# A parametric activation kept in its PSUM bank, and softmax maxima and sums that pass through PSUM columns

## Chip, cores and metric

One core of a Trainium2 chip runs the kernel. The metric is the device time of one execution in microseconds; 0.2% of it, some 1.7 us, is about what a measurement of this kernel can tell from no change.

The engines are named as the profile names them: PE is TensorE's matmuls, PEld its weight loads, DVE is VectorE, ACT is ScalarE, POOL is GpSimd, SP is SyncE, which here only issues DMAs.

## What is computed

Three stages follow each other on 2304 tokens (4 batches of 576) of 512 values, cut here to what matters:

```python
# 1. attention, 8 heads of 64; heads 0-3 see the last 32 keys, heads 4-7 every 32nd key
scores = scale * q @ k.T ; scores = where(mask, scores, -1e9)
attn = exp(scores - max(scores)) ; attn = attn / (sum(attn) + 1e-9) ; x = attn @ v
# 2. MLP, 512 -> 2048 -> 512, a slope alpha per hidden unit for negative values
h = x @ w_in ; g = maximum(h, 0) + alpha * minimum(h, 0) ; x = g @ w_out
# 3. eight routed experts, 512 -> 1024 -> 512, one expert per token by argmax of the gate
y = relu(x @ w1[e]) @ w2[e] ; out = gate * eom * y
```

## The kernel before

All products are made from fp32 values that are split into two float32r parts, high and low, so that each product is three matmuls (high x high, low x high, high x low).

**Attention.** 48 groups, 12 per batch, each of up to four score tiles ("units") of at most 128 by 128: two pairs of a row tile and a head for groups with 96 or 126 rows, two units for groups with 72 rows. `att_scores` (L218) writes the scores of one head of the pair to the half "S" of a bank and those of the other to another bank; S is columns 0 to 255 of the tile `sl_bank`, which is one PSUM bank of 512 columns. Its other half, "L", is used by the router (`rank`, L618). In the first two batches (`b < PE_MASK`, groups 0 to 23) the mask is added by a matmul and `att_max` (L252) reduces the scores in PSUM to negated maxima `nm`, four numbers a row in SBUF, which L255 multiplies in place by 0.125. In the last two batches (groups 24 to 47) the mask is added on DVE (L258) and the maxima come out of L266 ready. `att_exp` (L280) makes one exponential per unit on ACT, and its accumulator writes the row sums `sm` to SBUF. `att_norm` adds 1e-9 to them (L294), takes the reciprocal (L295), and GpSimd multiplies the tile by it (L296; for group 9 DVE does). Then come transposes (L312), their copy (L314), the product with v (L327) and the split of its result into the MLP's input (L366 on ACT, L371 on DVE).

**MLP.** Six blocks of 384 tokens, 16 pieces of 128 hidden units in each: 96 iterations n of a loop. Iteration n makes the first product of piece n+2 (`mlp_in`, 12 matmuls, L438 to L440, into one of two banks with the tag "h"), its activation (`mlp_act`) and, at its end, its split (`mlp_split`), and the second product of piece n (`mlp_out`, L473 to L475). The activation is two Relu on ACT out of PSUM, of h into `a` and of -h into `bn` (L447, L448, both SBUF), and one DVE instruction a = bn * (-alpha) + a (L449). The split is a copy to float32r on ACT (`gh`, L458) and the difference `gl` = a - gh (L460), on GpSimd in the first block (n < 16) and on DVE afterwards.

**Weights.** They come as float64 and are decoded by integer steps: a scaled copy on ACT (L401), a shift (L405), two shift-and-combine steps on DVE (L406, L412), a float32r copy on ACT (L420) and the difference on GpSimd (L421). 16 weights, five of them decoded beside the first ten attention groups, the rest one per iteration of the first block, for n up to 10.

**Order.** It is written by hand: each engine works through its own queue in program order. First comes a prologue, steps s = 0 to 12 of `att_step` (L1099): exponentials of group s-1, scores of group s (in S for even s, in the "h" banks for odd s), values of s-3, transposes of s-2, maxima of s, normalization of s-1, rest of s-3, then the decoding steps. Then the MLP loop; while it is in block 0 each iteration also holds one attention step (groups 10 to 22), in blocks 1 to 3 about one in two iterations does. Within an iteration the order is: exponentials and normalization of s-1, `mlp_in(n+2)`, values of s-3 and their store, rest, `mlp_act(n+2)`, the end of a decoding (L420, L421), scores and maxima of s, the middle of the next decoding (L405, L406, L412), `mlp_out(n)` with the transposes of s-2 in between, `mlp_split(n+2)`. Semaphores are placed by a framework from the tiles that instructions share. It keeps instructions of different engines on one tile of one PSUM bank in program order, whatever columns they touch: the router's product into columns 256 to 279 of `sl_bank` is given a wait for DVE's read of columns 0 to 255.

After the MLP the experts run (from about 560 us); the change does not touch them.

Of the kernel before, what the change touches and what calls it, by code (L numbers as in the profile page):

```python
# [7 lines left out]
F32 = mybir.dt.float32  # L8
# [4 lines left out]
ALU = mybir.AluOpType  # L13
# [35 lines left out]
SCALE = 0.125  # L49
# Splits ahead of the turn of the tokens of the place after next, by the kinds of three places in a row.  # L50
NB = {"SSP": 0}
XG = 4
XA = 3
# When the parts of the second plan, its lists and its indices come: (place, position).
WHEN = ((0, 7), (1, 1), (1, 1), (1, 4), (1, 6))
OHP = 12
# Groups that VectorE normalizes, and groups whose scores come after matmuls that keep TensorE awake.
NRV = (9,)
FS = {2: 2}
# Parts of the first two products of the MLP that run between the last steps of the first attention.  # L60
PRE = {10: ((0, range(2)),), 11: ((0, range(2, 3)), (1, range(2))), 12: ((1, range(2, 3)),)}
# [22 lines left out]
def attention_prelu_mlp_routed_experts_kernel(  # L84
# [40 lines left out]
    with tc.manual_schedule():  # L125
# [18 lines left out]

# [1 line left out]
        # A visit is a pair of heads of a batch and the groups of its rows that are worked on in turn.  # L146
        visits = [(0, pr, (0, 1) if pr < 2 else (0, 1, 2)) for pr in range(4)]
# [70 lines left out]
        def att_scores(gi, tags):  # L218
# [10 lines left out]
            for ii, j in enumerate(js):  # L229
                q0 = QL * j if local else NP * RS * j  # L230
                k0 = max(q0 - STRIDE, 0) if local else q0
                for h2 in range(2):
# [7 lines left out]
                    )  # L240

        def att_max(gi):
            b, pr, g = groups[gi]
            local, js, r, kk = shape_of(gi)
            nj = len(js)
            nu = 2 * nj
            sc = sc_t[gi]
            pt = apool.tile([P, 4, P], F32, tag="p", name="p", bufs=NP_BUFS)
            nm = apool.tile([P, 4], F32, tag="nm", name="nm", bufs=2)
            if b < PE_MASK:  # L250
                for h2 in range(2):
                    nc.vector.tensor_reduce(  # L252
                        out=nm[:r, h2 * nj : (h2 + 1) * nj], in_=sc[h2][:r, 0:nj, :kk], axis=X, op=ALU.max, negate=True
                    )
                nc.vector.tensor_scalar_mul(nm[:r, :nu], nm[:r, :nu], SCALE)  # L255
            else:
                for h2 in range(2):
                    nc.vector.scalar_tensor_tensor(  # L258
                        out=pt[:r, h2 * nj : (h2 + 1) * nj, :kk],
                        in0=sc[h2][:r, 0:nj, :kk],  # L260
                        scalar=SCALE,
                        in1=masks(gi),
                        op0=ALU.mult,
                        op1=ALU.add,
                    )
                nc.vector.tensor_reduce(  # L266
                    out=nm[:r, :nu], in_=pt[:r, :nu, :kk], axis=X, op=ALU.max, negate=True
                )
            p_t[gi] = (pt, nm)

        def att_exp(gi):
            b, pr, g = groups[gi]
            local, js, r, kk = shape_of(gi)
            nj = len(js)
            sc = sc_t.pop(gi)
            pt, nm = p_t[gi]
            sm = apool.tile([P, 4], F32, tag="sm", name="sm", bufs=3)
            for u in range(2 * nj):
                src = sc[u // nj][:r, u % nj, :kk] if b < PE_MASK else pt[:r, u, :kk]
                nc.scalar.activation(  # L280
                    out=pt[:r, u, :kk],
                    in_=src,
                    func=AF.Exp,
                    bias=nm[:r, u : u + 1],
                    scale=SCALE if b < PE_MASK else 1.0,
                    accum_out=sm[:r, u : u + 1],
                )
            p_t[gi] = (pt, sm)

        def att_norm(gi):  # L290
            local, js, r, kk = shape_of(gi)
            nu = 2 * len(js)
            pt, sm = p_t[gi]
            nc.vector.tensor_scalar_add(sm[:r, :nu], sm[:r, :nu], 1e-9)  # L294
            nc.vector.reciprocal(sm[:r, :nu], sm[:r, :nu])  # L295
            (nc.vector if gi in NRV else nc.gpsimd).tensor_tensor(  # L296
                out=pt[:r, :nu, :kk],
                in0=pt[:r, :nu, :kk],
                in1=sm[:r, :nu].unsqueeze(2).to_broadcast([r, nu, kk]),
                op=ALU.mult,  # L300
            )
# [72 lines left out]

# [1 line left out]
        raw_t, w_t = {}, {}  # L376
# [14 lines left out]

        # A weight comes as a float64, two words; it leaves as the sum of two float32r.
        dec_t = {}
# [48 lines left out]
        def mlp_act(n):  # L442
            c = n % NC1
            ph = h_t.pop(n)
            a = xpool.tile([P, BLK], F32, tag="a", name="a", bufs=2)
            bn = xpool.tile([P, BLK], F32, tag="bn", name="bn", bufs=1)
            nc.scalar.activation(out=a, in_=ph[:, :BLK], func=AF.Relu)  # L447
            nc.scalar.activation(out=bn, in_=ph[:, :BLK], func=AF.Relu, scale=-1.0)  # L448
            nc.vector.scalar_tensor_tensor(  # L449
                out=a, in0=bn, scalar=nalpha[:, c : c + 1], in1=a, op0=ALU.mult, op1=ALU.add  # L450
            )
            h_t[n] = a

        def mlp_split(n):
            a = h_t.pop(n)
            gh = xpool.tile([P, BLK], F32R, tag="gh", name="gh", bufs=3)
            gl = xpool.tile([P, BLK], F32R, tag="gl", name="gl", bufs=2)
            nc.scalar.activation(out=gh, in_=a, func=AF.Copy)  # L458
            eng = nc.gpsimd if n < NC1 else nc.vector
            eng.tensor_tensor(out=gl, in0=a, in1=gh.bitcast(F32), op=ALU.subtract)  # L460
            g_t[n] = (gh, gl)
# [16 lines left out]

# [1 line left out]
        x2_t, lg_t = {}, {}  # L480
# [77 lines left out]
        def route_parts(blk):  # L558
            """One-hot choice, weight and place in its expert's list of each token of a block."""
            lg = lg_t.pop(blk)  # L560
# [75 lines left out]
        def plan_parts(early):  # L636
            """A column is a list of up to 128 tokens of one expert, a place's tokens one or two columns. The
            first EARLY columns hold pairs of full lists of the tokens before the last block. The others
            of each expert come in pairs from C_P on, a last odd one from C_S on; but a last one of FEW
            tokens or less has its column from C_Q on."""  # L640
            k0, k1 = (0, EARLY) if early else (EARLY, NSLOT)
# [206 lines left out]

# [1 line left out]
        # A place is work on one expert: "P" on two columns, "S" on one, "Q" on one of few tokens. "P" makes  # L850
        # the hidden values with the tokens in the free dimension. "Q" takes the weights as they are, its
        # tokens stand in each quarter of the partitions, and each quarter makes its part of a row.
        kinds = ["P"] * (EARLY // 2)
# [13 lines left out]
        def load_expert(t, h, always=False):  # L867
            """The first (h = 0) or second weight of place t's expert, unless it is there already."""
            if t not in regs:
# [190 lines left out]

# [1 line left out]
        load_qk(0)  # L1062
# [36 lines left out]
        def att_step(s, tags, ttag, vtag):  # L1099
            """One step of the attention, each engine's part on what the others did a step ago."""  # L1100
            att_front(s)
# [20 lines left out]
        def decode(k, n):  # L1122
            """The first n steps of a weight's decoding, those that are still to be done."""
            steps = [decode_a, decode_b, decode_s, decode_c]
            for f in steps[steps_done.get(k, 0) : n]:
                f(k)
            steps_done[k] = max(steps_done.get(k, 0), min(n, 4))
# [36 lines left out]
        def gathers(ahead, places=NPL):  # L1164
            """The next tokens, as far as there is room for them."""
            ahead = ahead or len(xg_t) + 1
# [89 lines left out]

# [1 line left out]
        x2T = x2T_tile()  # L1258
# [20 lines left out]
        def split(t, h, some=range(4)):  # L1279
            """Splits, and loads what comes next in the place of what was split."""  # L1280
            if len(some) and t < NPL and kinds[t] != "Q":
# [102 lines left out]
        def some(kind, n, end, step):  # L1384
            """The places of a kind from the n-th on, as far as they are used, step by step."""
            if n < end:
# [105 lines left out]
```

## Time and profile before

| | us |
|---|---|
| three timed runs | 832.44, 833.76, 834.35 (median 833.76) |
| span of the profiled execution, first to last instruction | 831.9 |
| PE busy | 784.2 (94% of the span) |
| DVE, ACT, POOL busy | 478.4, 427.3, 244.5 |

The page gives no other time of the profiled execution than its span: the span lies 0.5 us below the fastest timed run and 1.9 us below the median. A busy time is the sum over an engine's instructions; an instruction that has started and waits for something inside the engine counts as busy. The share of 94% is an average: the first 160 us hold almost all of PE's idle time of the first two stages.

### The profile page before, as it was taken

How to read it: one execution, taken by the hardware profiler on the slowest of the kernel's cores; microseconds unless marked ns; L12 is line 12 of the kernel's file. 1: busy time of each engine (PE TensorE's matmuls, PEld its weight loads, DVE VectorE, ACT ScalarE, POOL GpSimd, SP SyncE). 2: the span in 40 equal slices, each digit the busy share in tenths (PEclk: the TensorE clock that was granted, in tenths of full speed). 3: DMA queues.
4: the chain of work that ended last, by engine and by line, in shares of the span. 5: the costliest groups of instructions: out<-in, count | busy, mean ns of one | idle time of the engine just before them, and what ended most of it. 6: DMA issues, size and time to landing. Idle time of an engine off the chain costs nothing. (4 is left out here: it accounts for less than half of the span.)

```text
span 831.9 us, 13663 instructions
## 1 busy us (share of the span) xinstructions
PE 784.2 (94%) x5032; PEld 659.6 (79%) x5035; DVE 478.4 (58%) x988; ACT 427.3 (51%) x1033; POOL 244.5 (29%) x168
## 2 busy tenths in 40 slices
PE   7687878999999999999999999999989998999995
PEld 4475766788888888888799898889878876878884
DVE  5989999345534554556333424757595447854422
ACT  6756665454455444665433333356534656655542
POOL 2756655200000000110000000032483354546422
PEclk9998999999999999999999999999999999999998
DMA  9716511101200121011000100362224577777421
GB/s 342 298 43 244 190 33 45 44 22 56 84 18 1 47 86 64 1 45 39 1 1 1 39 0 1 149 244 103 77 77 147 194 258 255 285 288 267 161 90 38
DMA packets 22621, 91.04 MB, mean 109 GB/s; under 512 B 3082, under 2 KB 7312, under 8 KB 15376
## 3 DMA queue, kind: packets, MB, share of 16 engines
q1 hardware_dynamic: 18816, 78.52, 26.6%
q0 software_dynamic: 3728, 11.55, 3.9%
q8 instruction: 41, 0.67, 0.3%
q14 instruction: 36, 0.29, 0.1%
HBM read 105.78 MB, written 9.97 MB: 139 GB/s over the span
## 5 line engine op out<-in xcount | busy, mean ns | idle before, releaser
L449 DVE SCALAR_TENSOR_TENSOR a<-bn,nalpha,a 128x384 f32<-128x384 f32 x96 | 73.2, 763 | 116.4 <-ACT bn L448 116.0
L438 PE MATMUL h<-xh,w 128*128 128x384 f32 x384 | 130.4, 340 | 0.4 <-ACT bn L448 0.4
L440 PE MATMUL h<-xh,w 128*128 128x384 f32 x384 | 129.9, 338 | 0.0
L439 PE MATMUL h<-xl,w 128*128 128x384 f32 x384 | 129.7, 338 | 0.0
L296 POOL TENSOR_TENSOR p<-p,sm 96x512 f32<-96x512 f32 (+2 forms) x47 | 48.7, 1036 | 267.6 <-DVE sm L295 255.3
L473 PE MATMUL acc<-w,gh 128*128 128x512 f32 x288 | 126.9, 441 | 0.0
L888 DVE TENSOR_TENSOR wx<-raw,wx 128x1024 fp32r<-128x1024 f32 x72 | 97.1, 1392 | 46.6 <-ACT wx L886 46.3
L475 PE MATMUL acc<-w,gl 128*128 128x512 f32 x288 | 115.8, 402 | 0.3 <-POOL gl L460 0.3
L474 PE MATMUL acc<-w,gh 128*128 128x512 f32 x288 | 115.6, 401 | 0.0
L886 ACT ACTIVATE wx<-raw 128x1024 fp32r<-128x1024 f32 x96 | 94.6, 1056 | 7.3 <-DMA raw<-in_wexp_dram 7.3
L447 ACT ACTIVATE a<-h 128x384 f32<-128x384 f32 x96 | 47.1, 491 | 99.7 <-PE h L440 99.6
L1042 PE MATMUL acc<-wx,hh 128*128 128x512 f32 x304 | 96.8, 400 | 0.0
L888 POOL TENSOR_TENSOR wx<-raw,wx 128x1024 fp32r<-128x1024 f32 x24 | 63.1, 2629 | 89.1 <-ACT wx L886 88.9
L438 PEld LDWEIGHTS h<-xh,w 128*128 128x128 f32 x384 | 73.1, 190 | 5.1 <-ACT bn L448 0.8
L439 PEld LDWEIGHTS h<-xl,w 128*128 128x128 f32 x384 | 72.9, 190 | 4.0
L440 PEld LDWEIGHTS h<-xh,w 128*128 128x128 f32 x384 | 72.6, 189 | 0.0
L895 POOL DMA_INDIRECT xg<-rows,idx_in x23 | 29.4, 1278 | 145.7 <-DVE a L449 139.3
L458 ACT ACTIVATE gh<-a 128x384 fp32r<-128x384 f32 x96 | 49.9, 520 | 42.6 <-DVE a L449 42.5
L475 PEld LDWEIGHTS acc<-w,gl 128*128 128x128 f32 x288 | 55.5, 193 | 14.2 <-POOL gl L460 0.8
L1042 PEld LDWEIGHTS acc<-wx,hh 128*128 128x128 f32 x304 | 56.5, 191 | 11.1
L473 PEld LDWEIGHTS acc<-w,gh 128*128 128x128 f32 x288 | 55.2, 192 | 11.1 <-issue 0.8
L460 DVE TENSOR_TENSOR gl<-a,gh 128x384 fp32r<-128x384 f32 x80 | 44.5, 556 | 28.7 <-ACT gh L458 16.6
(260 smaller groups left out, 1573.7 us busy)
## 6 DMA issues: line engine op xcount, KB each, us to landing
raw<-in_wexp_dram SPq DMA_DIRECT2D x64, 1024.0 KB
raw<-in_wp_dram SPq DMA_DIRECT2D x16, 1024.0 KB
qk<-in_qkv_dram SPq DMA_DIRECT2D x10, 576.0 KB
rows<-stage SPq DMA_DIRECT2D x15, 256.5 KB
v<-in_qkv_dram SPq DMA_DIRECT2D x8, 320.0 KB
qk<-in_qkv_dram SPq DMA_DIRECT2D x4, 384.0 KB
v<-in_qkv_dram SPq DMA_DIRECT2D x6, 256.0 KB
qk<-in_qkv_dram SPq DMA_DIRECT2D x4, 224.0 KB
```

Of the source, the lines that this page charges most:

```text
L296: (nc.vector if gi in NRV else nc.gpsimd).tensor_tensor(out=pt[:r, :nu, :kk], in0=pt[:r, :nu, :kk], in1=sm[:r, :nu].unsqueeze(2).to_broadc ...
L438: mm(ph[:, :BLK], w_in(c, 0, k), xh[:, k, :], start=(k == 0), stop=False)
L439: mm(ph[:, :BLK], w_in(c, 0, k), xl[:, k, :], start=False, stop=False)
L440: mm(ph[:, :BLK], w_in(c, 1, k), xh[:, k, :], start=False, stop=(k == KD - 1))
L449: nc.vector.scalar_tensor_tensor(out=a, in0=bn, scalar=nalpha[:, c : c + 1], in1=a, op0=ALU.mult, op1=ALU.add)
L458: nc.scalar.activation(out=gh, in_=a, func=AF.Copy)
L473: mm(o, gh[:, t], w_out(c, 0), start=(c == 0), stop=False)
L474: mm(o, gh[:, t], w_out(c, 1), start=False, stop=False)
L475: mm(o, gl[:, t], w_out(c, 0), start=False, stop=(c == NC1 - 1))
L886: nc.scalar.activation(out=w[:, :1024], in_=raw, func=AF.Copy)
L888: eng.tensor_tensor(out=w[:, 1024:], in0=raw, in1=w[:, :1024].bitcast(F32), op=ALU.subtract)
L1042: mm(po[i], h[:, h0 : h0 + P], wk[:, w0 : w0 + 512], start=st, stop=sp)
```

## The change

It does two things; beside them it only drops comment lines, so that line numbers stay.

1. In `mlp_act` and `mlp_split`, of -h the Relu writes back into the PSUM bank of h (`v`), the DVE instruction reads v from PSUM and a from SBUF and writes v again, and both steps of the split read v from PSUM. The tile `bn` is gone. The difference `gl` is made on DVE for all pieces. The bank of piece n is so in use until `gl` of piece n is made.
2. A function `few` gives each group four columns for its raw maxima (columns 448 to 479 of `sl_bank`, by group modulo 8) and four for its raw sums (columns 480 to 511). In the first two batches the reductions write there, and the scaling reads there and writes `nm` in SBUF. In all batches the exponentials' accumulators write the sums there, and the addition of 1e-9 reads there and writes `sm` in SBUF.

```diff
+        def few(gi, n):
+
+            c = 448 + 32 * n + 4 * (gi % 8)
+            return sl_bank[:, c : c + 4]
+
         def att_max(gi):
...
             if b < PE_MASK:
+                raw = few(gi, 0)
                 for h2 in range(2):
                     nc.vector.tensor_reduce(
-                        out=nm[:r, h2 * nj : (h2 + 1) * nj], in_=sc[h2][:r, 0:nj, :kk], axis=X, op=ALU.max, negate=True
+                        out=raw[:r, h2 * nj : (h2 + 1) * nj], in_=sc[h2][:r, 0:nj, :kk], axis=X, op=ALU.max, negate=True
                     )
-                nc.vector.tensor_scalar_mul(nm[:r, :nu], nm[:r, :nu], SCALE)
+                nc.vector.tensor_scalar_mul(nm[:r, :nu], raw[:r, :nu], SCALE)
...
-            sm = apool.tile([P, 4], F32, tag="sm", name="sm", bufs=3)
+            sm = few(gi, 1)
             for u in range(2 * nj):
...
-            pt, sm = p_t[gi]
-            nc.vector.tensor_scalar_add(sm[:r, :nu], sm[:r, :nu], 1e-9)
+            pt, raw = p_t[gi]
+            sm = apool.tile([P, 4], F32, tag="sm", name="sm", bufs=3)
+            nc.vector.tensor_scalar_add(sm[:r, :nu], raw[:r, :nu], 1e-9)
             nc.vector.reciprocal(sm[:r, :nu], sm[:r, :nu])
...
             ph = h_t.pop(n)
+            v = ph[:, :BLK]
             a = xpool.tile([P, BLK], F32, tag="a", name="a", bufs=2)
-            bn = xpool.tile([P, BLK], F32, tag="bn", name="bn", bufs=1)
-            nc.scalar.activation(out=a, in_=ph[:, :BLK], func=AF.Relu)
-            nc.scalar.activation(out=bn, in_=ph[:, :BLK], func=AF.Relu, scale=-1.0)
+            nc.scalar.activation(out=a, in_=v, func=AF.Relu)
+            nc.scalar.activation(out=v, in_=v, func=AF.Relu, scale=-1.0)
             nc.vector.scalar_tensor_tensor(
-                out=a, in0=bn, scalar=nalpha[:, c : c + 1], in1=a, op0=ALU.mult, op1=ALU.add
+                out=v, in0=v, scalar=nalpha[:, c : c + 1], in1=a, op0=ALU.mult, op1=ALU.add
             )
-            h_t[n] = a
+            h_t[n] = v
...
-            a = h_t.pop(n)
+            v = h_t.pop(n)
...
-            nc.scalar.activation(out=gh, in_=a, func=AF.Copy)
-            eng = nc.gpsimd if n < NC1 else nc.vector
-            eng.tensor_tensor(out=gl, in0=a, in1=gh.bitcast(F32), op=ALU.subtract)
+            nc.scalar.activation(out=gh, in_=v, func=AF.Copy)
+            nc.vector.tensor_tensor(out=gl, in0=v, in1=gh.bitcast(F32), op=ALU.subtract)
```

## Rows read from the trace of the kernel before

**Rows 1.** Busy time by stretch; per engine us and (instructions), then PEclk, DMA share, GB/s.

```profile
0.00:46.00 46.00, 33.57 (x245) 20.05 (x248) 35.25 (x83) 30.49 (x108) 21.98 (x17) 0.94 0.75 290
...
58.00:142.00 84.00, 68.10 (x389) 53.38 (x388) 82.39 (x107) 52.62 (x144) 49.83 (x31) 0.91 0.38 137
...
160.00:560.00 400.00, 399.37 (x2399) 343.59 (x2398) 190.58 (x536) 184.44 (x539) 31.45 (x31) 1.00 0.13 46
```

**Rows 2.** Groups of DVE instructions by line, 58 to 142 us: busy us, mean ns.

```profile
L406 DVE SCALAR_TENSOR_TENSOR stage<-raw,stage 128x1024 int32<-128x1024 int32 x11 | 21.8, 1982 | 0.4
L449 DVE SCALAR_TENSOR_TENSOR a<-bn,nalpha,a 128x384 f32<-128x384 f32 x11 | 18.3, 1665 | 0.2 <-issue 0.2
L255 DVE TENSOR_SCALAR nm<-nm 96x4 f32<-96x4 f32 (+2 forms) x10 | 16.9, 1692 | 0.3
```

**Rows 3.** Single lines over the whole span: durations in ns, minimum/median/maximum.

```profile
L371 DVE TENSOR_TENSOR xl<-T,xh x56: 168/323/358, 84.1 to 413.7; 128x192 fp32r<-128x192 f32 x20, 128x84 fp32r<-128x84 f32 x12, 128x168 fp32r<-128x168 f32 x12, 128x24 fp32r<-128x24 f32 x6
...
L460 DVE TENSOR_TENSOR gl<-a,gh x80: 546/558/560, 162.3 to 558.9; 128x384 fp32r<-128x384 f32 x80
...
L421 POOL TENSOR_TENSOR w<-stage,w x16: 2342/2582/3347, 23.5 to 142.2; 128x1024 fp32r<-128x1024 f32 x16
```

**Rows 4.** Timeline of one iteration of block 0, DVE and POOL: start, duration.

```profile
107.19 1.23 DVE L412 SCALAR_TENSOR_TENSOR stage<-raw,stage 128x1024 int32<-128x1024 int32 x1
108.33 0.17 DVE L294 TENSOR_SCALAR sm<-sm 126x4 f32<-126x4 f32 x1
...
108.86 1.03 POOL L296 TENSOR_TENSOR p<-p,sm 126x504 f32<-126x504 f32 x1 [3.58 <-DVE sm L295]
...
109.84 2.70 POOL L421 TENSOR_TENSOR w<-stage,w 128x1024 fp32r<-128x1024 f32 x1
...
110.99 1.58 DVE L255 TENSOR_SCALAR nm<-nm 126x4 f32<-126x4 f32 x1
...
112.48 0.68 DVE L405 TENSOR_SCALAR stage<-stage 128x1024 int32<-128x1024 int32 x1
...
112.69 1.35 POOL L460 TENSOR_TENSOR gl<-a,gh 128x384 fp32r<-128x384 f32 x1
...
113.20 1.92 DVE L406 SCALAR_TENSOR_TENSOR stage<-raw,stage 128x1024 int32<-128x1024 int32 x1
...
115.16 1.23 DVE L412 SCALAR_TENSOR_TENSOR stage<-raw,stage 128x1024 int32<-128x1024 int32 x1
```

**Rows 5.** Timeline: L412 of the sixth and of the sixteenth, last, weight.

```profile
58.88 1.92 DVE L412 SCALAR_TENSOR_TENSOR stage<-raw,stage 128x1024 int32<-128x1024 int32 x1
...
139.54 1.22 DVE L412 SCALAR_TENSOR_TENSOR stage<-raw,stage 128x1024 int32<-128x1024 int32 x1
```

**Rows 6.** One shape on DVE with a PSUM operand, from the groups by form: busy us, mean ns.

```profile
L500 DVE TENSOR_TENSOR x2hl<-T,x2hl 128x512 fp32r<-128x512 f32 x15 | 10.4, 692 | 11.7 <-ACT x2hl L499 11.7
```

**Rows 7.** Timeline of the prologue: first exponentials of groups 0, 1 and 4, a reduction, one step's scores.

```profile
7.72 0.75 DVE L252 TENSOR_REDUCE nm<-h 96x2 f32<-96x256 f32 x2
7.82 0.36 ACT L280 ACTIVATE p<-sl_bank,nm 96x128 f32<-96x128 f32 x1 [5.59 <-PE h L234]
...
9.20 0.36 ACT L280 ACTIVATE p<-h,nm 96x128 f32<-96x128 f32 x1
...
11.34 0.38 PE L228 MATMUL h<-cst 96*96 96x256 bf16 x2
...
11.65 0.68 PE L234 MATMUL h<-qk 64*96 64x128 f32 x8
...
19.43 0.37 ACT L280 ACTIVATE p<-sl_bank,nm 126x126 f32<-126x126 f32 x1
```

**Rows 8.** Timeline: first matmul of piece 2.

```profile
49.13 0.44 PE L438 MATMUL h<-xh,w 128*128 128x384 f32 x1 [0.44 <-ACT bn L448]
```

**Rows 9.** Timeline in block 3: sums of group 45 are read, scores of group 46 start.

```profile
390.60 0.17 DVE L294 TENSOR_SCALAR sm<-sm 126x4 f32<-126x4 f32 x1 [0.28 <-ACT p L280]
...
390.76 0.37 PE L234 MATMUL sl_bank<-qk 64*126 64x126 f32 x1
```

## The prediction

> **What bounds the kernel now.** I read the busy times by stretch first. From 160 to 560 us PE is busy 399.4 of 400 us and its granted clock is 1.00: a faster activation earns nothing there [rows 1]. From 58 to 142 us it is another kernel: DVE is busy 82.4 of 84 us, PE 68.1. So the groups of DVE in that stretch come next, and against them the single lines, which tell what an instruction takes when nothing hinders it. L255 handles four numbers a row and takes 1692 ns on average, L449 takes 1665 ns, L406 1982 ns [rows 2]. That is waiting inside the instruction, and the timeline of one iteration shows for what: L255 starts at 110.99 and ends at 112.57, just when GpSimd's L421 (109.84 + 2.70) ends; L406 at 113.20 sits behind GpSimd's L460 (112.69 + 1.35) [rows 4]. L371, with one operand in PSUM and one in SBUF, never takes over 358 ns while the same GpSimd work runs [rows 3]. So DVE instructions that read two SBUF tensors, or scale an SBUF tensor, and GpSimd's instructions shut each other out for their whole length, and a PSUM operand takes a DVE instruction out of that.
>
> The stretch is a loop through this lock. From one L412 to the next: norm after 1.14 us, L296 0.53 later, L421 0.98 later, L405 2.64 later, L406 0.72, L412 1.96: 7.97 us [rows 4]. Ten such pitches run from 58.88 to 139.54, 8.07 us each [rows 5].
>
> **Part 1, the loop of block 0.** L255, L294 and L449 leave the lock, and GpSimd loses L460. I redo the pitch. Added: `gl` now stands on DVE behind L412, 0.56 us [rows 3]. Kept: 1.14 + 0.53 + 0.98. L421 without a hindering L449 takes its minimum 2.34 [rows 3] in place of 2.64. L405 stays in the lock, and it comes right behind L255: what L255 waits for today, L405 waits for then. So L255's 1.69 us [rows 2] do not come free; this is the point where I depart from the plain sum of waits, which would be some 3 us an iteration. L405 to L406 0.72; L406 to L412 falls from 1.96 to 1.25, since no L460 stands in front. New pitch 1.14 + 0.56 + 0.53 + 0.98 + 2.28 + 0.72 + 1.25 = 7.46 us (2.28: L405's start lies 0.06 before L421's end). Against 7.97 that is 0.5, against the mean of 8.07 it is 0.6, as the longest pitches, where L449 lost the lock twice in a row, go too. Ten pitches: bounds 0 (every wait only changes place) and 16 (PE sets the pitch, below); I take 5.0, nearest to the chain.
>
> The DVE instructions on PSUM I cost like their SBUF forms: 692 ns for 512 elements out of PSUM against 558 ns for 384 out of SBUF is 134 ns for 128 elements, the slope alone [rows 3, 6]. The Trainium skill (Perfetto Trace Analysis, Optimizing Scalar/DVE Operations) speaks against the change here: it gives DVE about 60 ns of fixed overhead on SBUF and about 125 ns on PSUM. By it, four such instructions an iteration would cost an estimated 0.26 us, 2.6 us over ten, and half of the gain would be gone; the rows show no such step.
>
> **Part 2, the prologue.** `sl_bank` is one bank, and different engines on it go in program order. So today's freedom ends in three ways: maxima of s wait for the exponentials of s-1, exponentials of s for the reading of the sums of s-2, and for even s the scores of s for the exponentials of s-1. In front of those scores PE stands still, and behind them in its queue are values of s-3 and transposes of s-2. Today ACT goes from group 0 to group 1 without a gap, 7.82 to 9.20, so exponentials take 1.38 us [rows 7]. A reduction pair takes 0.75, scale and addition 0.17 each [rows 4, 7], scores 0.99 (11.34 to 12.33). An odd step then costs 1.38 + 0.75 + 0.17 + 0.17 and three handovers of some 0.05, 2.6 us, an even one 0.99 more, 3.6. Group 4's exponentials would start at 7.82 + 2.6 + 3.6 + 2.6 + 3.6 = 20.2 instead of 19.43, and ACT's copies for group 2 and weight 1, which follow PE's late transposes, push them toward 22: 1 to 3 us late. From there to 46 us DVE is already the busy engine (35.3 of 46 us over the whole prologue, most of the idle part before 15 us [rows 1]), and L255 and L294 no longer wait for GpSimd in it, so that the DVE work behind them goes on beside L421; that returns some 0.5 us three times. I take +2.0, bounds 0 and +4.
>
> **Part 3, the h banks.** `mlp_in(n+2)` now waits for `gl(n)` instead of `bn(n)`. In the loop `gl(n)` is made an iteration and more before that. Only at the entry is it late: piece 2 starts at 49.13, 0.44 us after waiting for `bn` [rows 8]; `gl(0)` comes some 2.9 us later, behind a DVE that is in L412 until 50.2. PE loses 2.9 us, DVE, which sets the pace, had idle time just there: +0.3, bounds 0 and +2.9.
>
> **Part 4, the end of the loop.** Today the scores of the last pitch begin before L412; then they wait for L294, which stands behind L412 and `gl`. From the last L412 on PE sets the pace, so its queue is about 1 us further behind; against that stands the last L449 long in the lock. +0.5, bounds -1 and +1.5.
>
> **Part 5, blocks 1 to 5.** Scores of s wait for L294 of s-1, 24 times. The tightest is group 46: scores start at 390.76, L294 ends at 390.77 [rows 9]; a handover is all it can lose. The copy `gh` and the two Relu are hidden (ACT is busy 184 of 400 us), and so is DVE (191). +0.3, bounds 0 and +1.
>
> **The sum.** 831.9 + (2.0 - 5.0 + 0.3 + 0.5 + 0.3) = 830.0 for the profiled execution, whose span lies 1.9 us under the median. Against the median of 833.76 that is 831.8 us, 0.23% faster: just past what a measurement tells.
>
> **The rivals.** *Nothing to measure.* Prologue at +3, loop at -4: between 832.1 and 835.4, say 833.5. For it speaks that gain and loss are both chains of five or ten links with sizes near each other; against it, that the lock rows are plain.
>
> *Slower: the shared bank costs more than the lock gives back.* Place: steps 2 to 8 of the prologue, where PE's scores, and with them values and transposes, stand behind ACT's exponentials. It decides if the delay is not made up by 46 us and L405 waits all that L255 waited. Price: +4.0 and +1.0 for entry and end, while `gl` on DVE (5.6 us for ten) eats most of what L406 gains (0.71 each): 833.8 + 4.0 + 1.0 - 1.5 = 837.3. For it: no row shows two engines of this kernel on one bank at a time, and the chain above is already longer than today's. The Trainium skill (PSUM — Partial Sum Buffer, PSUM bank collisions raise a hardware error) has the reason for such an order: two engines may not access one bank and quadrant at once, even at different columns. That no run can show here, since the order is built in.
>
> *Faster by far: PE sets the pitch.* If L405 mostly finds GpSimd idle, the pitch falls to PE's own work, 68.1 us in 84 / 8.07 = 10.4 pitches, 6.5 us. Ten times 1.57 is 15.7, less 3.1 elsewhere: 821. Against it: L421 starts 2.65 us after L412 and DVE needs about 2.9 us to reach L405.
>
> *The change does not do what it says:* L255 or L449 still wait with a PSUM operand. Then the loop loses 0.56 an iteration and keeps 1.0: the time of the first rival or a little over.
>
> **How the numbers follow.** Forecast 0.37, PE-bound 0.08: faster 0.45. No difference 0.28. Slower 0.27, the mechanism above for most of it. The range: from 827.0 (loop at -9 with the rest as summed) to 838.0 (the slower rival with its own spread); outside are most of the PE-bound case and the worst of the slower one. The forecast's own range is 827 to 832.
>
> **What would show it.** Right: L255, L294 and L449 at about 0.2, 0.2 and 0.6 us throughout block 0, L405 with waits of 1 to 2 us in their place (today it has none: 0.68), L406 near 1.25, the pitch from L412 to L412 about 7.5; the sixth L412 some 2 us later than 58.88, the last one about 3 us earlier than 139.54; in the prologue L228 on `sl_bank` waiting for L280 in every even step. Wrong: L405 without waits (then the gain is larger), the sixth L412 over 4 us late, or new PE idle time between 160 and 560 us, which today is 0.6.

## The result, and the profile after

The change made the kernel slower: 847.06 us (median of four runs, 845.39 to 848.30) against 834.06 for the kernel before; the ratio on record, which is not the quotient of the two medians, is 1.0145, 95% interval 1.011 to 1.0181. The forecast was 831.8 us in a range of 827 to 838. The profiled execution's span is 843.6 us, 11.7 over that of before.

One thing in the text ahead of the prediction has to be put right before the rows are read: the line numbers do not stay. The new function pushes what follows it down by six to seven lines. L252, L255, L280, L294 of before are L258, L261, L286, L301 after; L366 and L314 are L373 and L321; L401, L405, L406, L412, L421 are L408, L412, L413, L419, L428; L449 and L460 are L456 and L466, L438 is L445.

Busy time by stretch of the kernel after, as in [rows 1]:

```profile
0.00:46.00 46.00, 29.71 (x190) 16.99 (x191) 22.94 (x61) 23.96 (x82) 14.38 (x14) 0.80 0.70 259
...
58.00:142.00 84.00, 67.15 (x378) 55.83 (x379) 73.52 (x112) 54.01 (x139) 34.21 (x19) 0.90 0.35 129
...
160.00:560.00 400.00, 398.89 (x2410) 342.85 (x2409) 186.22 (x539) 184.04 (x544) 28.50 (x30) 1.00 0.12 43
```

In the first 46 us DVE is busy 22.9 us where it was 35.3, ACT 24.0, PE 29.7 at a granted clock of 0.80 (0.94 before): no engine is the busy one any more, so they wait for each other. From 160 us on nearly all is as before. The first product of piece 0 tells how long the prologue is; first the kernel before, then the kernel after (timeline):

```profile
39.70 0.43 PE L438 MATMUL h<-xh,w 128*128 128x384 f32 x1
```

```profile
52.89 0.67 PE L445 MATMUL h<-xh,w 128*128 128x384 f32 x1
```

That is 13.2 us, more than the whole loss. The sixth and the last weight of block 0, as in [rows 5]:

```profile
74.19 1.22 DVE L419 SCALAR_TENSOR_TENSOR stage<-raw,stage 128x1024 int32<-128x1024 int32 x1
...
150.20 1.23 DVE L419 SCALAR_TENSOR_TENSOR stage<-raw,stage 128x1024 int32<-128x1024 int32 x1
```

By their ends, ten pitches take 76.0 us, 80.0 before: block 0 did become faster, by 4.0. And its groups of DVE, 58 to 142 us, as in [rows 2]:

```profile
L412 DVE TENSOR_SCALAR stage<-stage 128x1024 int32<-128x1024 int32 x11 | 19.7, 1787 | 0.0
L413 DVE SCALAR_TENSOR_TENSOR stage<-raw,stage 128x1024 int32<-128x1024 int32 x11 | 15.6, 1418 | 0.4
...
L456 DVE SCALAR_TENSOR_TENSOR h<-h,nalpha,a 128x384 f32<-128x384 f32 x12 | 7.4, 618 | 4.5 <-ACT h L455 4.5
...
L261 DVE TENSOR_SCALAR nm<-sl_bank 126x4 f32<-126x4 f32 (+2 forms) x9 | 1.4, 159 | 0.3
```

L456 takes 618 ns (1665 as L449), L261 takes 159 (1692 as L255): both leave the lock as forecast. The Trainium skill (SBUF — State Buffer, Who interferes with whom) says the same: a DVE instruction with at most one SBUF input, outside the two-port modes, does not contend with GpSimd; the rows of L456 and L261 agree. L413, which still reads two SBUF tensors, takes 1418 (1982 as L406), now that GpSimd makes no `gl` in front of it. But L412, the shift that took 0.68 us in [rows 4], takes 1787 ns on average: it waits where L255 waited.

What happens in the prologue, from the timeline (first exponentials of groups 0, 1, 2 and 4, what stands between them, and what each waited for):

```profile
6.92 0.36 ACT L286 ACTIVATE p<-sl_bank,nm 96x128 f32<-96x128 f32 x1 [4.69 <-DVE nm L261]
...
8.74 0.96 DVE L258 TENSOR_REDUCE sl_bank<-h 96x2 f32<-96x256 f32 x2 [1.91 <-ACT p L286]
...
10.07 0.36 ACT L286 ACTIVATE p<-h,nm 96x128 f32<-96x128 f32 x1 [1.37 <-DVE sm L301]
...
11.91 0.37 PE L228 MATMUL sl_bank<-cst 96*96 96x256 bf16 x1 [4.78 <-ACT p L286]
...
14.77 0.15 DVE L301 TENSOR_SCALAR sm<-sl_bank 96x4 f32<-96x4 f32 x1
14.81 0.49 ACT L321 ACTIVATE ptt<-T 128x384 f32<-128x384 f32 x1 [2.96 <-PE T L319]
...
15.20 1.11 ACT L408 ACTIVATE stage<-raw 128x1024 f32<-128x1024 f32 x1
...
16.22 0.35 ACT L286 ACTIVATE p<-sl_bank,nm 96x128 f32<-96x128 f32 x1
...
24.09 0.15 DVE L301 TENSOR_SCALAR sm<-sl_bank 96x4 f32<-96x4 f32 x1
...
24.73 0.33 ACT L373 ACTIVATE xh<-acc 128x192 fp32r<-128x192 f32 x1 [3.60 <-PE acc L334]
...
25.37 0.49 ACT L321 ACTIVATE ptt<-T 128x384 f32<-128x384 f32 x1 [0.31 <-PE T L319]
...
25.90 1.16 ACT L408 ACTIVATE stage<-raw 128x1024 f32<-128x1024 f32 x1
...
26.96 0.36 ACT L286 ACTIVATE p<-sl_bank,nm 126x126 f32<-126x126 f32 x1
```

This is a circle. The maxima of group 1 (8.74) wait for the exponentials of group 0, though they read another bank; the exponentials of group 1 (10.07) wait for the addition of group 0; the scores of group 2 (11.91) have waited 4.78 us for the exponentials of group 1. And from the addition at 24.09 to the exponentials at 26.96 it is ACT's own queue that fills the time: a value copy that came late because PE's values stand behind the waiting scores, a copy of transposes, a weight's first step.

### The profile page after: what moved, and what is told of

It is laid out like the page before. It is cut to its first block, busy times and chain, and to the rows that moved or that the text cites. A ratio compares the mean times of both kernels' runs of the same rounds, so it can differ in the third digit from the quotient of the medians.

```text
span 843.6 us, 13718 instructions
## 1 busy us (share of the span) xinstructions
PE 787.6 (93%) x5035; PEld 663.7 (79%) x5035; DVE 463.5 (55%) x1004; ACT 431.8 (51%) x1033; POOL 220.3 (26%) x152
## 5 line engine op out<-in xcount | busy, mean ns | idle before, releaser
L445 PE MATMUL h<-xh,w 128*128 128x384 f32 x384 | 130.8, 341 | 3.9 <-DVE gl L466 3.9
L303 POOL TENSOR_TENSOR p<-p,sm 96x512 f32<-96x512 f32 (+2 forms) x47 | 45.8, 975 | 303.4 <-DVE sm L302 249.3
L456 DVE SCALAR_TENSOR_TENSOR h<-h,nalpha,a 128x384 f32<-128x384 f32 x96 | 60.0, 625 | 117.1 <-ACT h L455 117.0
L481 PE MATMUL acc<-w,gl 128*128 128x512 f32 x288 | 114.7, 398 | 0.0
L445 PEld LDWEIGHTS h<-xh,w 128*128 128x128 f32 x384 | 72.9, 190 | 8.7 <-DVE gl L466 4.6
L466 DVE TENSOR_TENSOR gl<-h,gh 128x384 fp32r<-128x384 f32 x96 | 53.3, 555 | 32.9 <-PE acc L481 19.2
L481 PEld LDWEIGHTS acc<-w,gl 128*128 128x128 f32 x288 | 54.8, 190 | 13.3
L465 ACT ACTIVATE gh<-h 128x384 fp32r<-128x384 f32 x96 | 46.8, 487 | 34.7 <-DVE h L456 34.6
```

Source lines behind the costliest of these rows:

```text
L445: mm(ph[:, :BLK], w_in(c, 0, k), xh[:, k, :], start=(k == 0), stop=False)
L456: nc.vector.scalar_tensor_tensor(out=v, in0=v, scalar=nalpha[:, c : c + 1], in1=a, op0=ALU.mult, op1=ALU.add)
L466: nc.vector.tensor_tensor(out=gl, in0=v, in1=gh.bitcast(F32), op=ALU.subtract)
L481: mm(o, gl[:, t], w_out(c, 0), start=False, stop=(c == NC1 - 1))
```

## The experiments

All runs in one table: when piece 0's first product starts, when the fifth, sixth and sixteenth second shift-and-combine (L412 of before) end, the mean of the ten pitches between the last two, when piece 16's first product starts (all us, from the timelines of single executions), and the median time with the ratio to the kernel before on the same chip. Beside them the kernel before took 834.06 to 836.24 us, by chip, so rows are best compared by their ratios.

| kernel | piece 0 | 5th | 6th | 16th | pitch | piece 16 | time, ratio (95%) |
|---|---|---|---|---|---|---|---|
| before | 39.7 | 50.2 | 60.8 | 140.8 | 8.00 | 157.8 | |
| after | 52.9 | 62.7 | 75.4 | 151.4 | 7.60 | 167.8 | 847.06, 1.0145 (1.011 to 1.0181) |
| e1, columns alone | 53.6 | 63.4 | 73.9 | 155.9 | 8.19 | 173.4 | 850.24, 1.0173 (1.0156 to 1.019) |
| e2, activation alone | 39.7 | 49.9 | 62.4 | 134.4 | 7.21 | 150.0 | 829.71, 0.9929 (0.991 to 0.9948) |
| e3, columns from group 10 | 39.8 | 50.2 | 63.0 | 136.3 | 7.33 | 155.7 | 833.38, 0.9968 (0.9953 to 0.9983) |
| e4, columns in the group's own bank | 40.5 | 50.2 | 62.6 | 138.9 | 7.63 | 157.0 | 834.46, 0.9981 (0.9969 to 0.9992) |
| e5, maxima alone | 41.0 | 51.2 | 63.6 | 137.0 | 7.34 | 152.3 | 829.39, 0.9917 (0.9892 to 0.9942) |
| e6, sums alone | 52.7 | 62.8 | 75.2 | 151.9 | 7.66 | 169.8 | 847.07, 1.0117 (1.0079 to 1.0154) |
| e7, values first | 56.3 | 66.1 | 78.5 | 154.8 | 7.62 | 172.8 | 848.94, 1.0149 (1.0125 to 1.0173) |
| e8, gl on DVE | 39.5 | 49.6 | 59.3 | 137.2 | 7.79 | 154.0 | 833.07, 0.9967 (0.995 to 0.9984) |
| e9, activation from PSUM | 40.0 | 50.2 | 62.6 | 138.7 | 7.62 | 154.7 | 832.65, 0.9961 (0.9946 to 0.9976) |
| e10, exponentials early | 50.3 | 61.2 | 72.8 | 147.3 | 7.46 | 165.4 | 845.1, 1.0114 (1.0085 to 1.0142) |
| e11, activation with a late entry | 39.2 | 49.4 | 59.0 | 132.4 | 7.33 | 149.2 | 826.81, 0.9885 (0.9858 to 0.9912) |

### e1: the columns alone

```diff
-            nc.scalar.activation(out=v, in_=v, func=AF.Relu, scale=-1.0)
+            nc.scalar.activation(out=bn, in_=ph[:, :BLK], func=AF.Relu, scale=-1.0)
...
+            eng = nc.gpsimd if n < NC1 else nc.vector
```

> The MLP as before, the PSUM columns as in the change. Three theories. Order: the loss is the program order of three engines on one bank during the prologue. Instruction: the loss is dearer instructions (the exponentials of one unit follow each other every 0.455 us where it was 0.345). Activation: the loss comes with the h banks held longer. Order and instruction both expect the whole loss of the prologue here (first product of piece 0 starts near 52.9 us as in the change, 39.7 before) and little of the loop's gain, since L405 only takes over the waits and gl stays on GpSimd: about 845 to 849 us. Activation expects 834 or less.

Measured 850.24 us, 1.2 over the range of order and instruction (the kernel before took 836.24 beside it), piece 0 at 53.6: the prologue's whole loss comes with the columns, and the theory of the h banks is out. Block 0 gains nothing from them (8.19 a pitch, 8.00 before). Its groups, 58 to 142 us, say why:

```profile
L412 DVE TENSOR_SCALAR stage<-stage 128x1024 int32<-128x1024 int32 x11 | 19.3, 1752 | 0.0
```

The shift behind L255 now waits what L255 waited.

### e2: the activation alone

```diff
-                raw = few(gi, 0)
...
-            sm = few(gi, 1)
+            sm = apool.tile([P, 4], F32, tag="sm", name="sm", bufs=3)
```

> The activation in PSUM as in the change, maxima and sums in SBUF as before. Order and instruction expect the prologue of before (piece 0 at 39.7 us, within 0.3) and a part of the loop's gain, since L449 and gl leave the lock while L255 and L294 stay in it: 1 to 3 us, so 831 to 833. Activation expects most of the loss, over 840.

Measured 829.71 us, 0.9929: better than both kernels and than any expectation. The groups of DVE, 58 to 142 us (lines as before):

```profile
L406 DVE SCALAR_TENSOR_TENSOR stage<-raw,stage 128x1024 int32<-128x1024 int32 x11 | 19.8, 1797 | 0.4
L255 DVE TENSOR_SCALAR nm<-nm 96x4 f32<-96x4 f32 (+2 forms) x11 | 18.1, 1644 | 0.4
...
L449 DVE SCALAR_TENSOR_TENSOR h<-h,nalpha,a 128x384 f32<-128x384 f32 x12 | 7.4, 614 | 0.3 <-ACT h L448 0.3
L405 DVE TENSOR_SCALAR stage<-stage 128x1024 int32<-128x1024 int32 x10 | 6.8, 680 | 0.0
```

L255 still waits (1644 ns), L405 does not (680), and the pitch is 7.21. Held against the kernel after, L255 and L405 have only changed roles.

### e3: the columns from group 10 on

```diff
         def few(gi, n):
+            if gi < FIRST + EXTRA:
+                return apool.tile([P, 4], F32, tag=("nm", "sm")[n], name="few", bufs=2 + n)
...
```

> The change, with maxima and sums of groups 0 to 9 (the prologue) in SBUF as before and those of groups 10 to 47 in the columns. Order and instruction expect piece 0 at 39.7 us and ten pitches of block 0 at 7.6 us as in the change (8.0 before): 4 to 5 us under the kernel before, 829 to 830. If the loop only looks faster in the change because the prologue left it late with more data at hand, it falls back to 8.0 and the time is 834.

Measured 833.38 us, 0.9968, over the 829 to 830 expected: the prologue of before and a pitch of 7.33, even under the 7.6 expected, but 3.7 us over e2, 5.7 by the spans of the profiled executions (832.9 and 827.2). The pitches explain 1.2 of these; most of the rest is the end of block 0, 19.4 us from the last weight's step to piece 16 where e2 has 15.5. Two stretches of the timeline show it, e2 first: the scores' mask (L228), the step L412 and the addition L294.

```profile
132.31 0.31 PE L228 MATMUL sl_bank<-cst 96*96 96x256 bf16 x1
...
133.22 1.23 DVE L412 SCALAR_TENSOR_TENSOR stage<-raw,stage 128x1024 int32<-128x1024 int32 x1
...
134.83 0.16 DVE L294 TENSOR_SCALAR sm<-sm 96x4 f32<-96x4 f32 x1
```

The same in e3 (L421 is that step, L303 the addition, L481 the second product):

```profile
135.05 1.23 DVE L421 SCALAR_TENSOR_TENSOR stage<-raw,stage 128x1024 int32<-128x1024 int32 x1
...
136.66 0.15 DVE L303 TENSOR_SCALAR sm<-sl_bank 96x4 f32<-96x4 f32 x1
...
136.86 0.37 PE L228 MATMUL sl_bank<-cst 96*96 96x256 bf16 x1 [2.04 <-DVE sm L303]
...
138.48 0.79 PE L481 MATMUL acc<-w,gh 128*128 128x512 f32 x1
```

In e2 the scores go ahead of L412; in e3 they wait 2.04 us for an addition that stands behind it. After that wait PE runs at its lower level: the granted clock is 0.50 from 138 to 143 us (0.66 on average from 138 to 146), and the matmul of 0.79 us takes 0.50 at full clock in e2.

### e4: the columns of an odd group in its own bank

```diff
+            bank_of[gi] = sc[0]
...
-            return sl_bank[:, c : c + 4]
+            return bank_of[gi][:, c : c + 4]
```

> The change, with the columns of an odd group of the prologue in the h bank that its own scores lie in, instead of sl_bank; even groups and all later ones as in the change. Every instruction and every PSUM access of the change is kept; only the order between neighbouring groups goes. Order expects the prologue near that of before (piece 0 at 39.7 to 41.5 us) and 829 to 832 in all. Instruction expects a prologue still late by ten groups times four units times 0.11 us, 4.4 us and more: piece 0 at 44 to 53 us, 834 to 847 in all.

Measured 834.46 us, piece 0 at 40.5: the prologue as order expects it, the time over its 829 to 832, as the loop and its end stay longer than in e2 (pitch 7.63, 18.0 us to piece 16). Every instruction of the change is there, its exponentials still follow each other every 0.45 us, and 12.4 of the prologue's 13.2 us are gone. The first exponential of group 1 and the mask of group 2's scores (lines three higher than after; the first exponential starts at 8.71, the last of the four ends at 10.4):

```profile
8.71 0.36 ACT L289 ACTIVATE p<-h,nm 96x128 f32<-96x128 f32 x1
9.05 0.27 PE L231 MATMUL sl_bank<-cst 96*96 96x256 bf16 x1 [1.82 <-DVE sm L304]
```

The scores of group 2 now start while group 1's exponentials run. So it was the order of the engines in the shared bank, across neighbouring groups. Its pitch of 7.63, with the same code in block 0 as e3, shows that a pitch depends by some 0.3 us on how the engines enter the loop; smaller differences between pitches are not read here.

### e5 and e6: maxima alone, sums alone

```diff
-            sm = few(gi, 1)
+            sm = apool.tile([P, 4], F32, tag="sm", name="sm", bufs=3)
...
```

```diff
-                raw = few(gi, 0)
+                raw = nm
```

> The change with only the maxima in the columns of sl_bank; the sums in SBUF as before. The order of the maxima ties DVE to the exponentials of an even group only, and the scores of an even group to the scaling of the group before. Order expects a small part of the prologue's loss: piece 0 at 40 to 44 us (39.7 before, 52.9 with the change). The end of block 0 keeps the form of the activation alone (piece 16 some 15.6 us after the last L412, 19.4 with the columns), since scores no longer wait for the addition. In all 830 to 834 us.

> The change with only the sums in the columns of sl_bank; the maxima in SBUF as before. The maxima alone (the run before this one with that part) left the prologue near that of before: piece 0 at 41.0 us. If the sums make the order, piece 0 starts at 48 to 53 us, the exponentials of one unit follow each other every 0.455 us (0.345 with the sums in SBUF), the end of block 0 is long (18 to 19 us from the last L412 to piece 16), and the time is 840 to 846 us. If it takes both, piece 0 starts before 45 and the time is under 837.

Maxima alone: 829.39 us (830 to 834 expected), piece 0 at 41.0, 15.2 us from the last step to piece 16. Sums alone: 847.07 us (840 to 846 expected; the kernel before took 836.14 beside it), piece 0 at 52.7, 18.0. The sums carry the order, in the prologue and at the end of block 0; the maxima cost 1.3 us in the prologue and bring no shorter pitch (7.34, e2 7.21). The sums also set the exponentials further apart. Two consecutive ones of one group, maxima alone:

```profile
7.44 0.36 ACT L286 ACTIVATE p<-sl_bank,nm 96x128 f32<-96x128 f32 x1 [5.20 <-DVE nm L261]
7.70 0.19 ACT L286 ACTIVATION_READ_ACCUMULATOR p<-sl_bank,nm 96x1 f32 x1
7.80 0.35 ACT L286 ACTIVATE p<-sl_bank,nm 96x128 f32<-96x128 f32 x1
```

and sums alone:

```profile
7.82 0.36 ACT L286 ACTIVATE p<-sl_bank,nm 96x128 f32<-96x128 f32 x1 [5.58 <-PE h L234]
8.08 0.15 ACT L286 ACTIVATION_READ_ACCUMULATOR p<-sl_bank,nm 96x1 f32 x1
8.27 0.36 ACT L286 ACTIVATE p<-sl_bank,nm 96x128 f32<-96x128 f32 x1
```

From one exponential to the next it is 0.45 us where it was 0.36. With the sums in SBUF the next one starts 0.09 us before the row that writes the accumulator ends, with the sums in PSUM 0.04 after its end. That is a wait and not a dearer instruction: by the semaphore fields of the traces, 157 of the 176 exponentials of the kernel after wait for a count that ACT's own accumulator rows raise, and none of the kernel before. The maxima do the same to the reductions; the second of a pair, in the kernel before and in the kernel after, 58 to 142 us:

```profile
L252 DVE TENSOR_REDUCE nm<-X 96x2 f32<-96x256 f32 (+2 forms) x10 | 3.7, 368 | 0.0
```

```profile
L258 DVE TENSOR_REDUCE sl_bank<-X 126x2 f32<-126x252 f32 (+2 forms) x9 | 3.5, 386 | 1.3 <-DVE sl_bank L258 0.5
```

It is released by the reduction before it on the same engine. So the order in the bank holds back instructions of one engine too.

### e7: values ahead of scores

```diff
-            if on(s):
-                att_scores(s, tags)
...
             if on(s - LT):
                 att_transpose(s - LT, ttag)
+            if on(s):
+                att_scores(s, tags)
```

> The change with one thing moved: in a step of the prologue PE makes the values of s-3 and the transposes of s-2 ahead of the scores of s, and no longer behind them. If the even steps take 6 to 7.6 us because ACT's copies (of transposes, of values, of a weight) come late behind PE's waiting scores and then stand in front of the next exponentials, each even step gets 1.5 to 2.5 us shorter and piece 0 starts at 42 to 47 us. If the chain of exponentials, scores, maxima alone makes the step, piece 0 stays at 52 to 53.

Measured 848.94 us, piece 0 at 56.3, later than with the change: it misses both expectations. Its timeline, at group 2:

```profile
12.38 0.90 PE L319 MATMUL T<-cst,p 96*128 96x96 f32 x4 [4.50 <-POOL p L303]
...
13.93 0.42 PE L228 MATMUL sl_bank<-cst 96*96 96x256 bf16 x1
...
17.10 0.36 ACT L286 ACTIVATE p<-sl_bank,nm 96x128 f32<-96x128 f32 x1 [2.28 <-DVE sm L301]
```

ACT's queue is indeed out of the way (the exponentials wait for the addition alone, and start 0.1 to 0.3 us after its end in every step), but the scores that start at 13.93 instead of 11.91 now stand behind transposes that wait for GpSimd. From first exponential to first exponential the even steps fall by 5.5 us together (as counted under e10), and the odd ones rise by 6.6. The run moved the wait, so it does not tell the two apart; e10 was made for that.

### e10: exponentials ahead of ACT's copies

```diff
-            if on(s - 1):
+            if s >= NPRO and on(s - 1):
                 att_exp(s - 1)
...
             if on(s - 1):
                 att_norm(s - 1)
+            if s < NPRO and on(s):
+                att_exp(s)
```

> The change with one thing moved: in the prologue the exponentials of s stand in ACT's queue right behind the normalization of s-1 in the same step, ahead of the rest of s-3 and of the weights' copies, and no longer at the start of the next step. If the even steps are long because ACT's copies stand between the addition and the exponentials (1.3 us at group 2, 2.7 us at group 4), they fall from 6.2 to 7.6 us to 4.8 to 6, and piece 0 starts at 45 to 50 us. If the order in the bank alone makes the step, piece 0 stays at 52 to 54.

Measured 845.1 us, piece 0 at 50.3: in the first theory's direction and just outside its numbers. From the first exponential of one group to that of the next, for the even groups 2, 4, 6, 8 and the odd groups 1, 3, 5, 7 (us, from the timelines):

| | to 2, 4, 6, 8 | to 1, 3, 5, 7 |
|---|---|---|
| before | 3.76, 4.52, 3.43, 3.51 | 1.38, 1.95, 3.91, 4.68 |
| after | 6.15, 7.61, 7.34, 6.19 | 3.15, 3.13, 3.47, 3.56 |
| e4 | 3.72, 4.70, 3.45, 3.26 | 1.68, 3.80, 3.26, 4.75 |
| e10 | 5.13, 6.25, 6.25, 5.41 | 3.16, 4.42, 4.60, 2.72 |

The even steps lose 4.2 us together, the odd ones take 1.6 back. Why no more goes is seen in this stretch:

```profile
24.58 0.15 DVE L301 TENSOR_SCALAR sm<-sl_bank 96x4 f32<-96x4 f32 x1
...
26.43 0.49 ACT L321 ACTIVATE ptt<-T 128x384 f32<-128x384 f32 x1 [0.84 <-PE T L319]
...
26.82 0.36 ACT L286 ACTIVATE p<-sl_bank,nm 126x126 f32<-126x126 f32 x1
```

From addition to exponentials it is still 2.2 us, because the copy of the transposes stays ahead of them and waits for PE, whose transposes stand behind the scores.

### e8 and e9: gl on DVE alone, L449 out of the lock alone

```diff
-            eng = nc.gpsimd if n < NC1 else nc.vector
-            eng.tensor_tensor(out=gl, in0=a, in1=gh.bitcast(F32), op=ALU.subtract)
+            nc.vector.tensor_tensor(out=gl, in0=a, in1=gh.bitcast(F32), op=ALU.subtract)
```

```diff
-            bn = xpool.tile([P, BLK], F32, tag="bn", name="bn", bufs=1)
+            bn = ph[:, :BLK]
```

> The kernel before with one thing changed: gl of the first block on DVE, out of SBUF. GpSimd loses its 16 L460; L449 and L255 still read SBUF and wait for it. The activation alone gains 0.8 us a pitch (7.20 against 8.00). If what counts is that GpSimd's gl no longer stands in front of L406, this has most of that: pitch 7.3 to 7.6, 829 to 832 us. If it is L449 that counts, the pitch stays at 7.8 to 8.2 and the time at that of before or above.

> The kernel before with one thing changed: of -h the Relu writes back into PSUM and L449 reads it there, but writes a in SBUF as before, and GpSimd makes gl as before. L449 is out of the lock, L460 stays in it. If L449 is what counts, the pitch falls to 7.3 to 7.6; if the longest pitches alone go (where L449 took 3.6 us), to 7.7 to 7.9; if gl counts, it stays at 8.0. The bank comes free after L449, so piece 2 starts up to 1 us later than before.

e8: pitch 7.79, 833.07 us; e9: 7.62, 832.65. Neither is the whole: 0.21 and 0.38 a pitch are 0.59 of the 0.79 that both have together in e2. The 0.21 lies within the 0.3 that e4 told not to read, so that e8's share rests on its time and on the rows below. The groups of DVE, 58 to 142 us, e8 and then e9:

```profile
L406 DVE SCALAR_TENSOR_TENSOR stage<-raw,stage 128x1024 int32<-128x1024 int32 x11 | 19.8, 1797 | 0.4
L449 DVE SCALAR_TENSOR_TENSOR a<-bn,nalpha,a 128x384 f32<-128x384 f32 x11 | 17.0, 1547 | 0.0
```

```profile
L406 DVE SCALAR_TENSOR_TENSOR stage<-raw,stage 128x1024 int32<-128x1024 int32 x11 | 23.2, 2111 | 0.4
...
L449 DVE SCALAR_TENSOR_TENSOR a<-h,nalpha,a 128x384 f32<-128x384 f32 x11 | 6.7, 608 | 0.2 <-issue 0.2
```

Taking GpSimd's gl away shortens L406 and leaves L449 in the lock; taking L449 out leaves L406 behind GpSimd's gl.

### e11: the activation alone, with pieces 0 and 1 in SBUF

```diff
+            v = bn = ph[:, :BLK]
+            if n < 2:
+                v, bn = a, xpool.tile([P, BLK], F32, tag="bn", name="bn", bufs=1)
```

> The activation in PSUM alone (no columns), but pieces 0 and 1 with a and bn in SBUF as before, gl on DVE. In the activation alone piece 2 started at 51.6 us (49.1 before, 48.1 with gl on DVE out of SBUF) and the sixth L412 ended at 62.4 (60.8, 59.3). If that entry is the price of the held h banks, piece 2 starts at 48 to 49 us, the sixth L412 ends at 59.3 to 60.8, the pitch stays at 7.2 and the time falls by 1.5 to 3 us under that of the activation alone: 0.989 to 0.991 of the kernel before. If PE makes it up later anyway, it stays at 0.993.

Measured 826.81 us, 0.9885 (0.9858 to 0.9912): the lowest ratio of all, just past the 0.989 expected and under the kernel before and the one after; its interval just overlaps that of e2. The first product of piece 2 in e2 and in e11:

```profile
51.61 0.63 PE L438 MATMUL h<-xh,w 128*128 128x384 f32 x1 [3.71 <-DVE gl L459]
52.68 0.52 PE L438 MATMUL h<-xh,w 128*128 128x384 f32 x1
```

```profile
47.81 0.44 PE L438 MATMUL h<-xh,w 128*128 128x384 f32 x1 [0.44 <-ACT bn L450]
48.44 0.33 PE L438 MATMUL h<-xh,w 128*128 128x384 f32 x1
```

PE's wait of 3.71 us at the entry is gone, and with it the stretch at the lower clock behind it (0.52 us a matmul, 0.33 in e11). The sixth step ends 3.3 us earlier than in e2. How much of this lasts the traces leave open: at piece 16 they show 0.8 us of it (149.2 against 150.0), since pitch and end of block 0 are longer here, and the two profiled spans are alike (827.8, e2 827.2).

## Why the prediction was wrong

It was wrong in direction and in size, and one term did it. Term by term, in us of the profiled executions:

| term | forecast | measured | how |
|---|---|---|---|
| part 2, prologue | +2.0 (0 to +4) | +12.4 | fifth L412 ends at 62.7, 50.2 before |
| part 3, entry | +0.3 (0 to +2.9) | +2.2 | fifth to sixth end: 12.8, 10.6 before |
| part 1, ten pitches | -5.0 (0 to -16) | -4.0 | 76.0, 80.0 before |
| part 4, end of block 0 | +0.5 (-1 to +1.5) | -0.6 | last L412 to piece 16: 16.4, 17.0 before |
| part 5, blocks 1 to 5 | +0.3 (0 to +1) | +0.5 | piece 16 to piece 95: 395.8, 395.3 before |
| the rest | 0 | +1.1 | from piece 95 on: 279.9, 278.8 before |

Together 11.7, summed before rounding. The last line is no effect of the change: over the thirteen kernels that stretch takes 278.8 to 282.8 us, and before had the shortest.

**Part 2 failed.** The place and the mechanism were named rightly, in the forecast and more so in the slower rival (steps 2 to 8, scores behind exponentials, values and transposes behind scores); e4 shows the order as the cause and e6 that the sums carry it. The size was wrong by a factor of six, in three places. First, the chain gave an even step 3.6 us and it took 6.2 to 7.6: the chain went from the addition straight to the exponentials. ACT's queue stands between them, 1.3, 2.7, 3.8 and 2.0 us from the end of the addition to the first exponential at groups 2, 4, 6 and 8; the forecast let those copies push group 4 once. e10 takes a part of that out and the even steps fall by 4.2. Second, the durations were those of the kernel before, while in the change they are longer: four exponentials 1.8 us and not 1.38 and a pair of reductions 0.96 and not 0.75, by the waits inside one engine that e5 and e6 show, and the scores of group 2 last 1.7 us (11.91 to 13.59) and not 0.99, since PE, which has stood still for 4.78 us, runs them at a granted clock of 0.50 (1.00 in the scores of before that the chain used). Third, the delay was to be made up by 46 us in DVE's busy time. There was no such cover: DVE fell to half busy in the first 46 us, and a delay in a circle of waits was not made up by slack on one engine. How the 12.4 us divide among the three was not measured. The sign of being wrong that the prediction set, a sixth step over 4 us late, came: 74.19 against 58.88.

**Part 1 was right in size and in who earns it.** Its chain gives the loop 0.36 us for L449 out of the lock and 0.15 for `gl` (0.71 less 0.56), both parts of the activation, and nothing for the columns. e9 and e8, which make the two alone, shorten the pitch by 0.38 and 0.21; that both together give 0.79 in e2 was not foreseen. That L405 would wait what L255 waits was right, and e1 against before and e3 against e2 show the columns earning nothing in the loop. Two prices held: GpSimd's L428 takes 2.36 to 2.43 us in nearly every pitch (2.34 was taken), and PSUM reads cost like SBUF ones: over all 96 instructions the median of L456 is 626 ns, that of L449 before 619. The rule of the Trainium skill that spoke against (Perfetto Trace Analysis, Optimizing Scalar/DVE Operations: some 65 ns more overhead on PSUM) is not seen in that instruction's rows.

**Part 3 was mis-sized.** The late gl(0) was foreseen with its 2.9 us, and then covered by DVE's idle time. PE waited 3.69 us for it in the kernel after (3.71 in e2) and ran the next product at the lower clock; e11, which takes the held bank away at the entry, has a median 9.3 us under that of the kernel before where e2 has 6.5; the traces show less of this gain, as said under e11.

**Part 4** came out within its bounds, and the wait that it described is there: the scores behind the last step wait 2.54 us for the addition in the kernel after, 2.04 in e3. **Part 5** was right.

So the order of the rivals was wrong: slower had 0.27, and its mechanism was the true one, though its price for the prologue, 4.0 us, was a third of what it cost. Had the even step been drawn with all instructions of ACT's queue in it, the sign would probably have turned: 9.8 us lie between addition and exponentials in the four even steps, against a forecast gain of 1.9 in all. One sum is off: by its own terms the range begins at 833.8 + 3.1 - 9 = 827.9 and not at 827.0, which changes nothing here.

What stays open is whether sums in a PSUM bank used by nothing else would be free. That was not tried, as all eight banks are in use here.

## What to carry to other kernels

A few spare columns of a PSUM bank are not free storage: with an order by bank like this one they tie together every engine that touches the bank, and a software pipeline over two groups becomes a circle. If small results go to PSUM, put them into the bank that their own group's data already order. When a chain is drawn through such a wait, put into it everything that stands ahead in each engine's queue, once for each turn, and look for what takes over a lock's wait when one instruction leaves it.

## What the runs showed of the hardware

Reading from PSUM cost DVE nothing that shows: the median of L456 is 626 ns, that of L449, out of SBUF, 619. Small results into PSUM look dearer at first sight: ACT's exponentials with an accumulator follow each other every 0.45 us when it goes to PSUM and every 0.34 to 0.36 when it goes to SBUF, and DVE's reductions of two heads start 0.53 us apart (13.69 and 14.22 in the kernel after) against 0.33 (135.84 and 136.17 in e2), at durations of 0.43 and 0.41. But the later one of each pair waits for a semaphore of the one before, as e5 and e6 show, so no run here shows a price of the write itself. And PE's waits cost more than their length: behind the 2.04 us in e3 the granted clock was 0.50 from 138 to 143 us, and behind the 3.71 us in e2 from 52 to 55, the lower of its two levels (1.2 and 2.4 GHz).
